# The outputs of 512-token tiles turned by VectorE and stored in pieces, gated by ScalarE when they come back

## The chip, the cores and the metric

The kernel runs on one core of a Trainium2 chip. The metric is the time of one launch on the device, in microseconds (us). Engines are named as in the profile: PE is TensorE's matmul, PEld its weight load, DVE VectorE, ACT ScalarE, POOL GpSimd and SP SyncE; a q behind a name (SPq) is that engine's own queue of instructions.

## The reference

A causal convolution along the sequence, done by Fourier transforms, and then a mixture of experts that takes one expert for each token:

```
x: 8 x 5696 x 128, h: 5696 x 128            # 45568 tokens in all
y = irfft(rfft(x, 2S) * rfft(h, 2S))[:, :S]  # per channel
logits = y @ w_gate + modality_bias[modality_id]
e_idx = argmax(logits); gate_w = softmax(logits)[e_idx]
for e in range(8):
    h = relu(y[e_idx == e] @ w1[e])          # 128 -> 1024
    out[e_idx == e] = gate_w * (h @ w2[e])   # 1024 -> 128
```

## The kernel before

The convolution is a chain of matmul stages (stage1, stage23, stage4). stage4 makes rows of y, works out expert and gate of each, and scatters every row with its gate and its token number to `rows` in HBM, sorted by expert. Tables (`table`) then cut these sorted rows into tiles: LEVELS comes out as 18, 18 and 45 tiles of 512 tokens (81 "big" tiles, three levels) and 23 slots for "small" tiles of 256 tokens, of which 20 always run and the last 3 only if they are needed.

`Moe.tiles` takes one tile after the other in steps: 8 steps for a big tile, 4 for a small one, each for 128 (big) or 256 (small) columns of the hidden layer. A step is `gemm1` (each product in three matmuls, high and low halves of the operands), ACT's relu into hh, DVE's rest into hl, and, two steps later (LAG = 2), `gemm2`, which sums into PSUM tile po. `prep` splits the next tile's input into mxh (ACT) and mxl (DVE). For a small tile PE first transposes the input into PSUM tile pxt; for nearly all big tiles DVE turns 32x32 blocks into mxt instead, and the load (four DMAs of 128-byte pieces) has put the blocks where they belong. `finish(t - 1)` runs at step 2 of tile t: PE transposes the output ot (copied from po by ACT) into pxt, DVE multiplies it by the gate into of. pxt is one buffer (the pool has bufs=1), for the transposes of `prep` and those of `finish`.

The first two levels run beside stage4 of the convolution, which still scatters rows on the same POOL queue, so their 36 tiles are not written out: `finish` stores them to `late` in HBM, and `bring` loads them back (tile ob) from tile 37 on. `scatter` sends 128 rows per DMA from POOL to the output, by token numbers in mmt or held; `evenly` spreads the scatters, one step at most one, each tied to the step's relu. Once the convolution has ended, `moe.alone` is set and the rest (from about tile 32 on) is recorded with PE in program order; SP is in program order all the while, and DVE, ACT and POOL go by the order that a scheduler chose.

SP issues weights (`load_weights`, three slots, only if the expert changes), inputs and stores in one queue. The input's gate and token numbers (mmt) have 5 buffers, and a buffer is free when the scatters that read their token numbers from it have landed.

Of the kernel before, what the change touches and what calls it, by code (L numbers as in the profile page):

```python
# [10 lines left out]
F32 = mybir.dt.float32  # L11
F32R = mybir.dt.float32r
BF16 = mybir.dt.bfloat16
# [46 lines left out]
LEVELS += ((NTOK - sum(LEVELS) * TS + E * (TSL - 1)) // TSL,)  # L60
NLAST = 3
NHELD = LEVELS[0] + LEVELS[1]
SMALL = LEVELS[3] - NLAST
EVEN = ((NHELD + LEVELS[2]) * NSUB + SMALL * TSL // 128) / (8 * (LEVELS[2] - 2) + 4 * (SMALL - 3))
JOBS = [(lv, j) for lv, n in enumerate(LEVELS) for j in range(n)]
OOB_ROW = 1 << 22
OOB_TOK = 1 << 20
# [24 lines left out]
def conv_moe(  # L92
# [234 lines left out]
    def stage4(g, sp, ps, psl, qa, qb, paced=False, late=None):  # L327
# [39 lines left out]
        for q0 in range(qa, qb, QB):  # L367
# [7 lines left out]
            for qi in range(QB):  # L375
                q = q0 + qi
                u = us.pop(q)
                load_u(q + 1)
                if not paced:
                    uh = sp.tile([128, 2, GC], F32R, name="uh")  # L380
                    ul = sp.tile([128, 2, GC], F32R, name="ul")
                    nc.scalar.copy(uh, u)
                    nc.vector.tensor_tensor(ul, u, uh.bitcast(F32), op=ALU.subtract)
                yield
                py = ps.tile([128, GC], F32, name="py")
                if paced:
# [12 lines left out]
                for b in range(GB):  # L399
                    nc.tensor.transpose(pt[:, b, :], ry[:, b, :], ident)  # L400
                if whole:
                    yt = sp.tile([128, GB, 128], F32, name="yt")
                    nc.scalar.copy(yt, pt)
                    yield
                    for b in range(GB):
                        t = qi * GB + b
                        nc.tensor.matmul(pl[:, t * E:(t + 1) * E], yt[:, b, :], wg, start=True, stop=True)  # L407
                else:
                    ys = [late.tile([128, GB, 128], BF16, name=f"ys{i}") for i in range(3)]
# [168 lines left out]
    class Moe:  # L578
        def __init__(self, wp, sp0, sp, pst, psh, pso):
            self.sp0, self.sp, self.pst, self.psh, self.pso = sp0, sp, pst, psh, pso  # L580
            self.slots = [wp[i].tile([128, 2, 2, FF], F32R, name=f"slot{i}") for i in range(NSLOT)]
            self.st, self.alone = {}, False
            self.outs = []
            self.tabs = {}
            self.held = wp[0].tile([128, NHELD, NSUB], I32, name="held")
            self.back, self.backs, self.credit = 0, [], 0.0

        def on_pe(self, t):
            return t < NPE or JOBS[t][0] == len(LEVELS) - 1
# [1 line left out]
        def load(self, t):  # L591
            lv, j = JOBS[t]
            tab, src = self.tabs[lv]
            ts = TSL if lv == len(LEVELS) - 1 else TS
            ns = ts // 128
            r0 = nc.sync.value_load(tab[0:1, j:j + 1], min_val=0, max_val=E * REGION)
            rt = self.sp0.tile([128, TS], F32, name="mrt", bufs=4)
            mt = self.sp0.tile([128, NSUB, 2], F32, name="mmt", bufs=5)
            if self.on_pe(t):
                nc.sync.dma_start(rt[:, :ts].rearrange("p (c d) -> p c d", d=D), src[bass.ds(r0, ts), :D].rearrange("(c p) d -> p c d", p=128))  # L600
            else:
                for j in range(0, D, BK):
                    nc.sync.dma_start(rt[j:j + BK, :ts].rearrange("p (n w) -> p n w", w=BK),
                                      src[bass.ds(r0, ts), j:j + BK].rearrange("(n p) w -> p n w", p=BK))
            nc.sync.dma_start(mt[:, :ns], src[bass.ds(r0, ts), D:].rearrange("(c p) w -> p c w", p=128))
            self.st[t] = {"rt": rt, "mt": mt, "ts": ts, "ns": ns}

        def load_weights(self, t):
# [6 lines left out]
        def prep(self, t):  # L615
            st = self.st[t]
            rt, ts, ns = st["rt"], st["ts"], st["ns"]
            xp, s = (self.sp, "") if t else (self.sp0, "0")
            if self.on_pe(t):
                px = self.pst.tile([128, NSUB, 128], F32, name="pxt")  # L620
                for c in range(ns):
                    nc.tensor.transpose(px[:, c, :], rt[:, c * D:(c + 1) * D], ident)
                pf = px.rearrange("p c t -> p (c t)")[:, :ts]
            else:
                pf = self.sp0.tile([128, TS], F32, name="mxt", bufs=1)[:, :ts]
                nc.vector.transpose(pf, rt[:, :ts])
            xh = xp.tile([128, TS], F32R, name="mxh" + s)
            xl = xp.tile([128, TS], F32R, name="mxl" + s)
            nc.scalar.copy(xh[:, :ts], pf)
            nc.vector.tensor_tensor(xl[:, :ts], pf, xh[:, :ts].bitcast(F32), op=ALU.subtract)  # L630
            st.update(xh=xh[:, :ts], xl=xl[:, :ts])

        def gemm1(self, t, f):
            w = self.slots[t % NSLOT]
# [16 lines left out]
        def gemm2(self, t, f):  # L651
# [13 lines left out]
                nc.tensor.matmul(po, w[:, 1, 1, fs], hh[:, cs], start=False, stop=False)  # L665
                nc.tensor.matmul(po, w[:, 1, 0, fs], hl[:, cs], start=False, stop=k == 7)  # L666
            if k == 7:
                ot = self.sp.tile([128, TS], F32, name="ot")
                nc.scalar.copy(ot[:, :ts], po)
                st["ot"] = ot  # L670

        def finish(self, t):
            st = self.st.pop(t)
            ns = st["ns"]
            pq = self.pst.tile([128, NSUB, 128], F32, name="pxt")
            for c in range(ns):
                nc.tensor.transpose(pq[:, c, :], st["ot"][:, c * 128:(c + 1) * 128], ident)  # L677
            of = self.sp.tile([128, NSUB, D], F32, name="of")
            rt = st["mt"]
            nc.vector.tensor_tensor(of[:, :ns], pq[:, :ns], rt[:, :ns, 0:1].to_broadcast([128, ns, D]), op=ALU.mult)  # L680
            ri = rt.bitcast(I32)
            if t < NHELD:
                nc.gpsimd.tensor_copy(self.held[:, t, :].unsqueeze(2), ri[:, :, 1:])
                nc.sync.dma_start(late_d[t], of.rearrange("p c d -> p (c d)"))
                return
            for c in range(ns):
                self.outs.append((t, c, ri[:, c, 1:2], of))

        def bring(self):
            if self.back < NHELD and len(self.backs) <= NSUB // 2:  # L690
                t = self.back
                self.back += 1
                of = self.sp.tile([128, NSUB, D], F32, name="ob")
                nc.sync.dma_start(of.rearrange("p c d -> p (c d)"), late_d[t])
                for c in range(NSUB):
                    self.backs.append((t, c, self.held[:, t, c:c + 1], of))

        def evenly(self, after):
            self.credit = min(self.credit + EVEN, 1.5)
# [24 lines left out]
        def tiles(self, first, total):  # L724
# [11 lines left out]
            for g in range(len(steps) + LAG):  # L736
# [5 lines left out]
                if t < total:  # L742
# [1 line left out]
                    dispatch(1, self.st[t]["act"])  # L744
                    self.evenly(self.st[t]["act"])
                    if t > NHELD:
                        self.bring()
                else:
                    self.scatter(1)
                if g >= LAG:  # L750
# [14 lines left out]
            while self.outs or self.backs or self.back < NHELD:  # L765
                self.scatter(len(self.outs))
                self.outs, self.backs = self.backs, []
                self.bring()
# [11 lines left out]
    with tc.tile_pool(name="p4l", bufs=1, space=PSUM) as ps4l:  # L780
# [19 lines left out]
        with tc.tile_pool(name="moe", bufs=2) as sp, tc.tile_pool(name="moew", bufs=1) as wp, \  # L800
# [120 lines left out]
```

## Time and profile before

| | us |
|---|---|
| median of 3 runs (2046.9 to 2052.02) | 2047.59 |
| the profiled execution's own time | 2045.59 |
| its span in the trace | 2043.8 |
| PE busy | 1962.4 (96%) |
| DVE busy | 1445.8 (71%) |
| ACT busy | 1133.6 (55%) |
| POOL busy | 1112.3 (54%) |

The tiles begin at about 808 us. The convolution ends at about 1350, big tiles at 1904, and the last matmul starts at 2031. Times in the trace count from the span's start. A matmul's duration covers its way through the array, and the next one starts before it ends; so what a matmul costs is read from one start to the next.

### The profile page before, as it was taken

How to read it: one execution, taken by the hardware profiler on the slowest of the kernel's cores; microseconds unless marked ns; L12 is line 12 of the kernel's file. 1: busy time of each engine (PE TensorE's matmuls, PEld its weight loads, DVE VectorE, ACT ScalarE, POOL GpSimd, SP SyncE). 2: the span in 40 equal slices, each digit the busy share in tenths (PEclk: the TensorE clock that was granted, in tenths of full speed). 3: DMA queues.
4: the chain of work that ended last, by engine and by line, in shares of the span. 5: the costliest groups of instructions: out<-in, count | busy, mean ns of one | idle time of the engine just before them, and what ended most of it. 6: DMA issues, size and time to landing. Idle time of an engine off the chain costs nothing. (4 is left out here: it accounts for less than half of the span.)

```text
span 2043.8 us, 32620 instructions
## 1 busy us (share of the span) xinstructions
PE 1962.4 (96%) x9114; PEld 1418.1 (69%) x9114; DVE 1445.8 (71%) x2478; ACT 1133.6 (55%) x2000; POOL 1112.3 (54%) x1085
## 2 busy tenths in 40 slices
PE   6889999999999899899999999999999999999996
PEld 5755555544544445778878778788888888888996
DVE  7759888886787897577676776866666666666553
ACT  5756777644444444566566666555555555555553
POOL 2117777673777685444444444633555555555554
PEclk8989999999999998999999999999999999999998
DMA  9998999979999997644456644354333343334443
GB/s 332 403 354 286 330 325 326 299 237 325 331 336 322 308 328 240 187 133 133 104 168 173 177 125 101 80 173 92 78 77 78 79 116 81 76 80 150 149 152 121
DMA packets 395832, 407.09 MB, mean 199 GB/s; under 512 B 242584, under 2 KB 277369, under 8 KB 393345
## 3 DMA queue, kind: packets, MB, share of 16 engines
q1 hardware_dynamic: 324496, 271.97, 44.7%
q10 hardware_dynamic: 47920, 85.94, 13.1%
q0 software_dynamic: 23232, 47.08, 6.7%
q8 instruction: 74, 1.21, 0.2%
q14 instruction: 110, 0.89, 0.1%
HBM read 396.70 MB, written 182.99 MB: 284 GB/s over the span
## 5 line engine op out<-in xcount | busy, mean ns | idle before, releaser
L320 POOL DMA_INDIRECT rows<-rt,idx x360 | 369.2, 1025 | 271.1 <-ACT hh L647 184.0
L648 DVE SCALAR_TENSOR_TENSOR hl<-ph,hh 128x512 fp32r<-128x512 f32 x496 | 338.0, 684 | 211.7 <-ACT hh L647 205.7
L647 ACT ACTIVATE hh<-ph 128x512 fp32r<-128x512 f32 x496 | 295.7, 598 | 278.3 <-PE ph L644 234.1
L290 POOL TENSOR_TENSOR t<-t,t 96x512 f32<-96x512 f32 x224 | 328.7, 1487 | 140.5 <-DVE t L283 119.9
L283 DVE TENSOR_TENSOR t<-px,hs 96x512 f32<-96x512 f32 x512 | 318.2, 676 | 68.3 <-PE px L280 29.5
L709 POOL DMA_INDIRECT out<-of,mmt x220 | 216.8, 985 | 216.4 <-ACT hh L647 186.7
L664 PE MATMUL po<-hh,slot 128*128 128x512 f32 (+1 forms) x808 | 304.3, 377 | 7.0 <-ACT hh L647 6.9
L666 PE MATMUL po<-hl,slot 128*128 128x512 f32 (+1 forms) x808 | 300.3, 372 | 0.3 <-DVE hl L648 0.3
L665 PE MATMUL po<-hh,slot 128*128 128x512 f32 (+1 forms) x808 | 299.5, 371 | 0.0
L280 PE MATMUL px<-z,m 96*96 96x512 f32 x512 | 256.1, 601 | 5.7 <-DMA z<-z 2.7
L648 DVE SCALAR_TENSOR_TENSOR hl<-py,hh 128x512 fp32r<-128x512 f32 x232 | 160.0, 690 | 105.2 <-ACT hh L647 105.0
L647 ACT ACTIVATE hh<-py 128x512 fp32r<-128x512 f32 x232 | 138.5, 597 | 164.2 <-PE py L644 152.1
L263 ACT COPY ut<-pu 90x512 f32<-90x512 f32 x256 | 147.9, 580 | 137.2 <-PE pu L258 69.1
L642 PE MATMUL ph<-mxh,slot 128*128 128x512 f32 (+1 forms) x536 | 210.7, 393 | 4.6 <-SPq L720 3.8
L258 PE MATMUL pu<-t,mi 96*96 96x512 f32 x384 | 199.0, 610 | 7.9 <-ACT ut L263 4.6
L644 PE MATMUL ph<-mxl,slot 128*128 128x512 f32 (+1 forms) x536 | 201.9, 377 | 0.0
L643 PE MATMUL ph<-mxh,slot 128*128 128x512 f32 (+1 forms) x536 | 201.9, 377 | 0.0
L709 POOL DMA_INDIRECT out<-ob,held x144 | 139.9, 971 | 109.6 <-ACT hh L647 90.6
L664 PEld LDWEIGHTS po<-hh,slot 128*128 128x128 f32 x808 | 152.8, 189 | 35.2 <-ACT hh L647 9.8
L666 PEld LDWEIGHTS po<-hl,slot 128*128 128x128 f32 x808 | 152.5, 189 | 28.3 <-DVE hl L648 0.9
L665 PEld LDWEIGHTS po<-hh,slot 128*128 128x128 f32 x808 | 152.8, 189 | 25.1
L280 PEld LDWEIGHTS px<-z,m 96*96 96x96 f32 x512 | 82.4, 165 | 119.8 <-issue 72.9
(173 smaller groups left out, 3464.0 us busy)
## 6 DMA issues: line engine op xcount, KB each, us to landing
slot<-w12s SPq DMA_DIRECT2D x101, 2048.0 KB
z<-z SPq DMA_DIRECT2D x128, 360.0 KB
z<-z SPq DMA_DIRECT2D x45, 640.0 KB
z<-z SPq DMA_DIRECT2D x45, 512.0 KB
mrt<-rows SPq DMA_DIRECT2D x312, 64.0 KB
w12s<-ws ACTq DMA_DIRECT2D x32, 512.0 KB
u<-ua ACTq DMA_DIRECT2D x63, 256.0 KB
u<-ub ACTq DMA_DIRECT2D x63, 256.0 KB
```

Of the source, the lines that this page charges most:

```text
L280: nc.tensor.matmul(px[:KP], mm, zbuf[k % NZ][:, i], start=True, stop=True)
L283: prods[0] = nc.vector.tensor_tensor(prod[i, j].rearrange("p (b d) -> p b d", d=D), px[:KP].rearrange("p (b d) -> p b d", d=D), hs[:, j, k ...
L290: add = eng.tensor_tensor(y[:, i], y[:, i], prod[1, 1 - i], op=ALU.add if i else ALU.subtract)
L320: d = nc.gpsimd.indirect_dma_start(views[count[0] % NVIEW], bass.IndirectOffsetOnAxis(ap=idx[:, t:t + 1], axis=0), rt[:, t, :], None, boun ...
L642: nc.tensor.matmul(po, w[:, 0, 0, fs], st["xh"], start=True, stop=False)
L643: nc.tensor.matmul(po, w[:, 0, 1, fs], st["xh"], start=False, stop=False)
L647: st["act"] = nc.scalar.activation(hh, ph, AF.Relu)
L648: nc.vector.scalar_tensor_tensor(hl, ph, 0.0, hh.bitcast(F32), op0=ALU.max, op1=ALU.subtract)
L664: nc.tensor.matmul(po, w[:, 1, 0, fs], hh[:, cs], start=k == 0, stop=False)
L665: nc.tensor.matmul(po, w[:, 1, 1, fs], hh[:, cs], start=False, stop=False)
L666: nc.tensor.matmul(po, w[:, 1, 0, fs], hl[:, cs], start=False, stop=k == 7)
L709: d = nc.gpsimd.indirect_dma_start(oviews[(t * NSUB + c) % NVIEW], bass.IndirectOffsetOnAxis(ap=ix, axis=0), of[:, c, :], None, bounds_che ...
```

## The change

The output of every big tile now goes through `late`, and PE transposes none of them. After the last `gemm2` of a big tile DVE turns po in 32x32 blocks into ot (one buffer), and `finish` stores ot with four DMAs, each of 32 partitions and 16 x 32 pieces of 128 bytes, so that `late` holds whole token rows. `bring` loads whole tiles back into the buffers that stage4 used for ys (four of them), and `gate` lets ACT multiply one block of 128 rows a step by its gate, in place, from 8 steps after the load was asked for. Gate and token numbers of big tiles stay in the tiles near and held; those of small tiles have 8 buffers. Small tiles are finished as before. When the tiles run alone, `prep` is cut into `turn`, `high` and `low`, recorded in three steps that follow each other, and DVE and ACT keep program order too.

```
+            near = wp[0].tile([128, NEAR, NSUB, 2], F32, name="near")
+            held = sp.tile([128, NBIG - NEAR, NSUB, 2], F32, name="held", bufs=1)
+            self.meta = [near[:, t] if t < NEAR else held[:, t - NEAR] for t in range(NBIG)]
...
-            mt = self.sp0.tile([128, NSUB, 2], F32, name="mmt", bufs=5)
+            mt = self.meta[t] if t < NBIG else self.sp0.tile([128, TSL // 128, 2], F32, name="mmt", bufs=8)
...
             if k == 7:
-                ot = self.sp.tile([128, TS], F32, name="ot")
-                nc.scalar.copy(ot[:, :ts], po)
-                st["ot"] = ot
+                ot = st["ot"] = self.sp.tile([128, TS], F32, name="ot", bufs=1)[:, :ts]
+                if t < NBIG:
+                    nc.vector.transpose(ot, po)
+                else:
+                    nc.scalar.copy(ot, po)
 
         def finish(self, t):
             st = self.st.pop(t)
             ns = st["ns"]
+            if t < NBIG:
+                for j in range(0, D, BK):
+                    nc.sync.dma_start(late_d[t].rearrange("(n p) d -> p n d", p=BK)[:, :, j:j + BK],
+                                      st["ot"][j:j + BK].rearrange("p (n w) -> p n w", w=BK))
+                return
             pq = self.pst.tile([128, NSUB, 128], F32, name="pxt")
...
+        def bring(self, t):
+            if self.back < min(NBIG, t - 1) and len(self.ripe) + len(self.backs) < (NOB - 1) * NSUB:
+                yb = self.sp.tile([128, 3, GB, 128], BF16, name="ys", bufs=NOB)
+                ob = yb.rearrange("p i b t -> p (i b t)").bitcast(F32)[:, :TS].rearrange("p (c d) -> p c d", d=D)
+                nc.sync.dma_start(ob.rearrange("p c d -> p (c d)"), late_d[self.back].rearrange("(p c) d -> p (c d)", c=NSUB))
+                self.ripe += [[AGE, self.back, c, ob] for c in range(NSUB)]
                 self.back += 1
...
+        def gate(self, after=None):
+            for it in self.ripe:
+                it[0] -= 1
+            while self.ripe and (after is None or self.ripe[0][0] < 0):
+                _, t, c, ob = self.ripe.pop(0)
+                mt = self.meta[t]
+                m = nc.scalar.activation(ob[:, c], ob[:, c], AF.Copy, scale=mt[:, c, 0:1])
+                self.backs.append((t, c, mt.bitcast(I32)[:, c, 1:2], ob))
+                if after is not None:
+                    tc.add_manual_dep(m.ins, after.ins.name, PACED, reason="order")
+                    break
...
                 if t + 1 < total:
-                    if f == (4 if n == 8 else 0):
-                        self.prep(t + 1)
+                    parts = (self.turn, self.high, self.low)
+                    if not self.alone:
+                        if f == (4 if n == 8 else 0):
+                            self.prep(t + 1)
+                    elif f - (3 if n == 8 else 0) in range(3):
+                        parts[f - (3 if n == 8 else 0)](t + 1)
...
-            with tc.manual_schedule(engines={mybir.EngineType.PE}):
+            with tc.manual_schedule(engines={mybir.EngineType.PE, mybir.EngineType.Activation, mybir.EngineType.DVE}):
                 run_all((tiles, 1))
```

How it stands on three engines (rows of before carry its line numbers, rows of the changed kernel its own). First PE at step 2 of a big tile that runs alone, from `gemm1` (into ph) over `gemm2` (into po) to the next step's `gemm1` (into py). Before:

```order
L642 MATMUL ph_22789<-mxh_22681,slot2_7161 128x512
L643 MATMUL ph_22789<-mxh_22681,slot2_7161 128x512
L644 MATMUL ph_22789<-mxl_22682,slot2_7161 128x512
L664 MATMUL po_22800<-hh_22728,slot2_7161 128x512
L665 MATMUL po_22800<-hh_22728,slot2_7161 128x512
L666 MATMUL po_22800<-hl_22729,slot2_7161 128x512
L677 MATMUL pxt_22804<-ident_67,ot_22752 128x128 x4
L642 MATMUL py_22811<-mxh_22681,slot2_7161 128x512
```

The same place in the changed kernel:

```order
L660 MATMUL ph_22364<-mxh_22251,slot0_7159 128x512
L661 MATMUL ph_22364<-mxh_22251,slot0_7159 128x512
L662 MATMUL ph_22364<-mxl_22252,slot0_7159 128x512
L682 MATMUL po_22378<-hh_22303,slot0_7159 128x512
L683 MATMUL po_22378<-hh_22303,slot0_7159 128x512
L684 MATMUL po_22378<-hl_22304,slot0_7159 128x512
L660 MATMUL py_22386<-mxh_22251,slot0_7159 128x512
```

The four transposes of the tile before are gone, and nothing stands in their place.

Next DVE over one small tile. hl are the steps' rests, mxl the low half of the next tile's input (read from pxt, where PE's `turn` of step 0 put it), of the gated output of the tile before (read from pxt, too). Before, from one mxl to the next:

```order
L630 TENSOR_TENSOR mxl_25009<-pxt_25005,mxh_25008 128x256
L648 SCALAR_TENSOR_TENSOR hl_25020<-py_25012,hh_25019 128x512
L648 SCALAR_TENSOR_TENSOR hl_25076<-ph_25068,hh_25075 128x512
L680 TENSOR_TENSOR of_25092<-pxt_25089,mmt_24562 128x256
L648 SCALAR_TENSOR_TENSOR hl_25102<-py_25094,hh_25101 128x512
L648 SCALAR_TENSOR_TENSOR hl_25122<-ph_25114,hh_25121 128x512
L630 TENSOR_TENSOR mxl_25135<-pxt_25131,mxh_25134 128x256
```

And in the changed kernel, from the hl of step 3 to the hl of step 3 of the next tile:

```order
L666 SCALAR_TENSOR_TENSOR hl_23783<-py_23775,hh_23782 128x512
L666 SCALAR_TENSOR_TENSOR hl_23803<-ph_23795,hh_23802 128x512
L666 SCALAR_TENSOR_TENSOR hl_23823<-py_23815,hh_23822 128x512
L666 SCALAR_TENSOR_TENSOR hl_23881<-ph_23873,hh_23880 128x512
L644 TENSOR_TENSOR mxl_23871<-pxt_23812,mxh_23870 128x256
L705 TENSOR_TENSOR of_23899<-pxt_23896,mmt_23353 128x256
L666 SCALAR_TENSOR_TENSOR hl_23909<-py_23901,hh_23908 128x512
```

mxl stood behind the hl of step 0 and now stands behind the hl of step 2, directly ahead of of; PE's transposes for of stand at the end of step 2 in both kernels, and write the pxt that mxl reads.

Last POOL at its end, ahead of the branch to the three slots that may not be needed (of are blocks of small tiles, ob and ys those of big ones). Before:

```order
L709 DMA out<-of_25672,mmt_25189 45568x128
L709 DMA out<-ob_25403,held_7162 45568x128 x2
L709 DMA out<-of_25760,mmt_25316 45568x128 x2
L709 DMA out<-of_25802,mmt_25442 45568x128 x2
L719 TENSOR_LOAD tab3_15729
```

And in the changed kernel:

```order
L741 DMA out<-of_25716,mmt_25266 45568x128 x2
L741 DMA out<-ys_25103,held_7163 45568x128
L741 DMA out<-ys_24722,held_7163 45568x128 x2
L741 DMA out<-of_25758,mmt_25391 45568x128 x2
L741 DMA out<-ys_25103,held_7163 45568x128 x2
L751 TENSOR_LOAD tab3_15492
```

Two blocks of a big tile now stand behind the last small tile's two.

## Rows read from the trace of the kernel before

**Rows 1.** The page's first part: busy time, share of the span and instructions.

```profile
PE 1962.4 (96%) x9114; PEld 1418.1 (69%) x9114; DVE 1445.8 (71%) x2478; ACT 1133.6 (55%) x2000; POOL 1112.3 (54%) x1085
```

**Rows 2.** Busy time by stretch, then PE's granted clock, DMA share, GB/s.

```profile
830.00:1350.00 520.00, 518.11 (x2833) 417.56 (x2833) 374.22 (x804) 322.73 (x581) 260.51 (x304) 1.00 0.51 138
1350.00:1904.00 554.00, 553.68 (x2525) 454.54 (x2524) 348.03 (x530) 284.78 (x484) 290.08 (x297) 1.00 0.39 95
1904.00:2014.00 110.00, 109.46 (x925) 109.26 (x924) 62.90 (x107) 55.21 (x106) 56.53 (x59) 1.00 0.50 161
```

**Rows 3.** Timeline of PE in a big tile: start, duration, what.

```profile
1501.66 0.39 PE L666 MATMUL po<-hl,slot 128*128 128x512 f32 x1
1501.89 0.60 PE L677 MATMUL pxt<-ident,ot 128*128 128x128 f32 x4
1502.24 0.48 PE L642 MATMUL py<-mxh,slot 128*128 128x512 f32 x1
1502.56 0.39 PE L643 MATMUL py<-mxh,slot 128*128 128x512 f32 x1
```

**Rows 4.** The chain that ended last: start, us, what; 43 tiles' transposes, first, last.

```profile
1410.19 0.44 PE pxt L677 x4
...
1891.88 0.44 PE pxt L677 x4
```

**Rows 5.** Timeline of all engines in a small tile.

```profile
1988.75 0.42 DVE L630 TENSOR_TENSOR mxl<-pxt,mxh 128x256 fp32r<-128x256 f32 x1
...
1990.17 0.28 PE L644 MATMUL ph<-mxl,slot 128*128 128x256 f32 x1
...
1990.49 0.60 ACT L647 ACTIVATE hh<-ph 128x512 fp32r<-128x512 f32 x1 [0.35 <-PE ph L644]
...
1991.02 0.38 PE L677 MATMUL pxt<-ident,ot 128*128 128x128 f32 x2
...
1991.13 0.69 DVE L648 SCALAR_TENSOR_TENSOR hl<-ph,hh 128x512 fp32r<-128x512 f32 x1 [0.75 <-ACT hh L647]
```

**Rows 6.** Timeline of PE around its two gaps among the small tiles.

```profile
1985.56 0.28 PE L666 MATMUL po<-hl,slot 128*128 128x256 f32 x1
1986.38 0.39 PE L642 MATMUL ph<-mxh,slot 128*128 128x256 f32 x1 [0.54 <-DMA slot<-w12s]
1986.61 0.28 PE L643 MATMUL ph<-mxh,slot 128*128 128x256 f32 x1
...
2017.16 0.28 PE L666 MATMUL po<-hl,slot 128*128 128x256 f32 x1
2021.27 0.58 PE L642 MATMUL ph<-mxh,slot 128*128 128x256 f32 x1 [3.82 <-SPq L720]
...
2024.63 0.31 PE L642 MATMUL py<-mxh,slot 128*128 128x256 f32 x1
```

**Rows 7.** Timeline of SP's queue: one input of a big tile; the last weights.

```profile
1501.57 1.93 SPq L603 DMA_DIRECT2D mrt<-rows  x4
...
2010.22 0.38 SPq L605 DMA_DIRECT2D mmt<-rows  x1
2012.50 0.35 SPq L613 DMA_DIRECT2D slot<-w12s  x1
```

**Rows 8.** SP's waits, 1904 to 2034 us: us in total, times, longest.

```profile
SPq L605 <- DMA out<-of,mmt: 27.3, 12, 6.4
```

**Rows 9.** Groups by shape, 1060 to 2044 us: count, busy us, mean ns, idle before.

```profile
L626 DVE STREAM_TRANSPOSE mxt<-mrt 128x512 f32<-128x512 f32 x64 | 44.9, 702 | 2.2 <-DMA mrt<-rows 2.1
L451 ACT ACTIVATE ex<-lg 128x96 f32<-128x96 f32 x10 | 2.9, 295 | 1.0 <-DVE lg L436 0.9
```

**Rows 10.** Timeline of POOL at its end.

```profile
2032.05 0.97 POOL L709 DMA_INDIRECT out<-of,mmt  x1 [0.72 <-DVE of L680]
2033.33 0.97 POOL L709 DMA_INDIRECT out<-of,mmt  x1 [0.30 <-issue]
```

**Rows 11.** DMA queues, 1400 to 1900 us: packets, MB, share of 16 engines.

```profile
q1 hardware_dynamic: 114454, 25.46, 27.0%
```

More of the change, by code (lines that the diff above doesn't have):

```diff
@@ L62 @@
 NHELD = LEVELS[0] + LEVELS[1]
+NBIG = NHELD + LEVELS[2]
+NEAR = 4
+AGE = 7
+NOB = 4
 SMALL = LEVELS[3] - NLAST
-EVEN = ((NHELD + LEVELS[2]) * NSUB + SMALL * TSL // 128) / (8 * (LEVELS[2] - 2) + 4 * (SMALL - 3))
+EVEN = (NBIG * NSUB + SMALL * TSL // 128) / (8 * (LEVELS[2] - 2) + 4 * (SMALL - 3))
 JOBS = [(lv, j) for lv, n in enumerate(LEVELS) for j in range(n)]
@@ L408, in stage4 @@
                 else:
-                    ys = [late.tile([128, GB, 128], BF16, name=f"ys{i}") for i in range(3)]
+                    yb = late.tile([128, 3, GB, 128], BF16, name="ys", bufs=NOB)
+                    ys = [yb[:, i] for i in range(3)]
                     yr = sp.tile([128, GB, 128], F32, name="yt")
@@ L584, in __init__ @@
             self.tabs = {}
-            self.held = wp[0].tile([128, NHELD, NSUB], I32, name="held")
-            self.back, self.backs, self.credit = 0, [], 0.0
+            near = wp[0].tile([128, NEAR, NSUB, 2], F32, name="near")
+            held = sp.tile([128, NBIG - NEAR, NSUB, 2], F32, name="held", bufs=1)
+            self.meta = [near[:, t] if t < NEAR else held[:, t - NEAR] for t in range(NBIG)]
+            self.back, self.ripe, self.backs, self.credit = 0, [], [], 0.0
         def on_pe(self, t):
@@ L622, in prep, with high, low @@
                     nc.tensor.transpose(px[:, c, :], rt[:, c * D:(c + 1) * D], ident)
-                pf = px.rearrange("p c t -> p (c t)")[:, :ts]
+                st["pf"] = px.rearrange("p c t -> p (c t)")[:, :ts]
             else:
-                pf = self.sp0.tile([128, TS], F32, name="mxt", bufs=1)[:, :ts]
+                pf = st["pf"] = self.sp0.tile([128, TS], F32, name="mxt", bufs=1)[:, :ts]
                 nc.vector.transpose(pf, rt[:, :ts])
[L627 to L631, printed above, removed]
+        def high(self, t):
+            st = self.st[t]
+            xp, s = (self.sp, "") if t else (self.sp0, "0")
+            st["xh"] = xp.tile([128, TS], F32R, name="mxh" + s)[:, :st["ts"]]
+            st["xl"] = xp.tile([128, TS], F32R, name="mxl" + s)[:, :st["ts"]]
+            nc.scalar.copy(st["xh"], st["pf"])
+        def low(self, t):
+            st = self.st[t]
+            nc.vector.tensor_tensor(st["xl"], st["pf"], st["xh"].bitcast(F32), op=ALU.subtract)
+        def prep(self, t):
+            self.turn(t)
+            self.high(t)
+            self.low(t)
         def gemm1(self, t, f):
@@ L677, in finish @@
                 nc.tensor.transpose(pq[:, c, :], st["ot"][:, c * 128:(c + 1) * 128], ident)
-            of = self.sp.tile([128, NSUB, D], F32, name="of")
+            of = self.sp.tile([128, TSL // 128, D], F32, name="of")
             rt = st["mt"]
-            nc.vector.tensor_tensor(of[:, :ns], pq[:, :ns], rt[:, :ns, 0:1].to_broadcast([128, ns, D]), op=ALU.mult)
+            nc.vector.tensor_tensor(of, pq[:, :ns], rt[:, :ns, 0:1].to_broadcast([128, ns, D]), op=ALU.mult)
             ri = rt.bitcast(I32)
[L682 to L685, printed above, removed]
@@ L686, in finish @@
             for c in range(ns):
                 self.outs.append((t, c, ri[:, c, 1:2], of))
-        def bring(self):
-            if self.back < NHELD and len(self.backs) <= NSUB // 2:
-                t = self.back
-                self.back += 1
[L693 to L696, printed above, removed]
+        def bring(self, t):
[4 more added lines that the diff above has]
+                self.ripe += [[AGE, self.back, c, ob] for c in range(NSUB)]
+                self.back += 1
@@ L746, in tiles @@
                     if t > NHELD:
-                        self.bring()
+                        self.gate(self.st[t]["act"])
+                        self.bring(t)
                 else:
@@ L764, in tiles @@
                 self.finish(total - 1)
-            while self.outs or self.backs or self.back < NHELD:
+            while self.outs or self.backs or self.ripe or self.back < NBIG:
                 self.scatter(len(self.outs))
+                self.gate()
                 self.outs, self.backs = self.backs, []
-                self.bring()
+                self.bring(total)
     fx = ExitStack()
@@ L914 @@
     args.append(scratch("w12s", (E, 128, 2, 2, FF)))
-    args.append(scratch("late", (NHELD, 128, TS)))
+    args.append(scratch("late", (NBIG, TS, D)))
     args.append(nc.dram_tensor("out", (NTOK, D), F32, kind="ExternalOutput").ap())
```

6 lines of the change are left out of this document (3 added, 3 removed).

## The prediction

> **What bounds the kernel now.** I read the page's busy times first: PE is busy for 96% of the span, no other engine for more than 71% [rows 1]. As a busy PE need not be a PE at its peak, the table by stretch comes next: beside the convolution, in the big tiles that run alone and in the small tiles PE has at most 0.4% idle, at a granted clock of 1.00, the 2.4 GHz level [rows 2]. So from 830 us to 2014 us the end is set by the list of PE's instructions, and the reader is to see that an instruction taken off that list is worth its full pitch until something new makes PE wait. The pitch is in the timeline: in a big tile L677's four transposes start 0.23 us after the matmul ahead of them, and the second matmul behind them starts 0.67 us after they do, where 0.23 is usual; so the four cost 0.44 us [rows 3]. The chain of waits gives the same 0.44 to each, and a period of (1891.88 - 1410.19) / 42 = 11.47 us a tile [rows 4]; the other 48 matmuls at 0.23 make 11.04.
>
> **What goes.** 81 big tiles lose these transposes: 81 x 0.44 = 35.6 us (28 if only the distance to the next matmul's start, 0.35, is saved; 38 at 0.47).
>
> **What the big tiles get in exchange.** DVE turns po instead of multiplying: the block transpose of an input of the same size takes 0.70 us [rows 9]; the place of the multiplication is free for it. ACT gets one gating of 128x128 a step and loses the copy of ot. Such a gating isn't in the trace; 128x96 takes 0.295 us [rows 9], so I take 0.3, with 0 and the 0.60 of a 128x512 relu [rows 5] as its ends. A step lasts 11.47 / 8 = 1.43 us and holds one relu, 0.60 + 0.30 of ACT's time, and even 1.20 fits. In program order each DVE step carries hl (0.69) and at most one more instruction of 0.70, 1.39 in a step of 1.43 (1.38 without the transposes); a surplus of 0.01 passes on to the next step, which carries hl alone, and hl is wanted two steps later; that hides it. SP issues four more DMAs a tile, 1.93 us by the four of an input [rows 7], and one to two loads; it has about 3 us of work in 11.47. The pieces of a store are as small as those of an input. Queue q1's packets took 27.0% of 16 engines over 500 us, 114454 of them: 0.27 x 500 x 16 / 114454 = 18.9 ns each [rows 11]. A store of 2048 pieces then takes 2048 x 18.9 ns / 16 = 2.4 us of the 16 DMA engines (nothing to 4.8 us if a written piece costs twice). The mean DMA share of 0.39 is 4.5 us a tile [rows 2]; with 2.4 and about 1 us more of loads it is 7.9 of 11, so the stores stay hidden. What is left are three or four weight loads between the big tiles, behind which a load of ys can be late and hold ACT at its gate, and the start of the stage alone: 0 to 6 us, I take 1.
>
> **What the small tiles get.** Here the order matters more than the work. pxt is one buffer. Before, DVE read its share of it at 1988.75 to 1989.17, and PE wrote the finished tile's transposes into it at 1991.02, straight behind its matmuls [rows 5]. In the changed order mxl stands behind step 2's hl, and PE's transposes, at the end of the same step, must wait for mxl. The same rows give the times: that step's last `gemm1` matmul starts at 1990.17, hh follows at 1990.49, hl at 1991.13 and takes 0.69, then mxl 0.42: 1992.24, against 1991.02. PE waits 1.2 us in each tile where `low` of the next and `finish` of a small one meet, tiles 82 to 99: 18 x 1.2 = **21.6 us** lost (20 if DVE overlaps the two, 29 if ACT's gate, ot and mxh delay hh by 0.4; nothing if I misread the order). Behind PE's transposes stand all later matmuls, so nothing covers it; ACT and DVE then wait for those.
>
> **What SP gives back.** PE has two gaps among the small tiles, both at weights. Matmuls follow each other at 0.12; from 1985.56 to 1986.38 there are 0.7 us too many, from 2017.16 to 2021.27 there are 4.0 [rows 6]. The weights of the second were issued at 2012.50, 2.3 us behind an mmt load [rows 7] which waits for scatters; such waits cost SP 27.3 us in 12 times, up to 6.4 [rows 8]. With 8 buffers for small tiles alone they go, and the longer tiles give the weights two times 1.2 us more. From 2021.27 to 2024.63 PE starts 15 matmuls, 0.22 each where 0.12 is usual: the level of 1.2 GHz, 3.36 - 15 x 0.12 = 1.6 us. Together 0.7 + 4.0 + 1.6 = 6.3 us returned (bounds 0 and 6.3).
>
> **The tail.** In the new POOL order two blocks stand behind the last small tile's. POOL's last scatters start 1.28 apart [rows 10]: 2.6 us. Up to eight blocks of big tiles have no step to pace them, so the bounds are 0 and 10.
>
> **The sum.** 2045.6 (the profiled execution's own time) - 35.6 + 1 + 21.6 - 6.3 + 2.6 = 2028.9. The median of the runs shown is 2.0 above that execution, so **2031 us**; its own range is 2020 to 2041. That is 0.8% less, half of what the removed transposes alone would bring. 0.3% of 2047.59 is 6.1 us, about what a measurement of this kernel can tell from no change.
>
> **Rivals.**
>
> *No wait at pxt.* If mxl is done in time after all, the 21.6 stays: 2045.6 - 35.6 + 1 - 5 + 2.6 + 2.0 = **2011**. For it: DVE is busy for only 62.9 of 110 us there [rows 2], and mxh is ready a step earlier. Against it: program order leaves DVE no choice, and hl cannot start ahead of hh. Chance 0.22.
>
> *The pieces are too slow* (slower than before). ot has one buffer, and DVE may not write it until the store has read it, 11 us later. SP issues the store behind the input's DMAs, some 6 us after the tile's last matmul, which leaves about 5 us for 2.4. Up to twice the price per piece, 4.8, nothing happens; at 8 us DVE would come 3 us late in 49 tiles alone, less 1.5 of slack: 2031 + 73 = **2104**. A gain of 16.8 is used up when each of the 49 loses 0.34 us, at a store of about 7 us. For it: no row has a written piece of 128 bytes. Against it: read pieces and the rest of q1 average 18.9 ns [rows 11]. Chance 0.08. The Trainium skill speaks against this step of the change: DMA: Bandwidth & Descriptors, Specifications, puts the least transfer for line rate at 512 bytes and says that below this the DMA does a read-modify-write. By that rule a written piece would cost more than a read one; at twice, an estimate from that page's words, the store takes 4.8 us and the sum stays as it is, and no run here shows the price.
>
> *The clock falls among the small tiles.* A small tile is 4 steps of 12 matmuls at 0.12, 5.8 us, and two pairs of transposes, some 6.1; a wait of 1.2 us per tile takes PE to 84% busy. After the 4 us gap the clock was halved and 1.6 us were lost; after the 0.7 us gap the matmul behind the next started 0.23 later and the pace was 0.12 again [rows 6]. If each of the 18 waits cost half clock as the long gap did: 2031 + 18 x 1.6 = **2060**; 0.9 us per wait takes the gain away. Chance 0.10.
>
> *Late loads.* If the back-loads come late often and ACT's gate holds hh, or the stores disturb the stage beside the convolution (DMA share 0.51 [rows 2]), 5 to 20 us are lost: about **2043**. Chance 0.08.
>
> **How the numbers follow.** The forecast has 0.52; the four rivals have 0.22, 0.08, 0.10 and 0.08. The range from 2007 to 2044 takes in the first rival, the forecast and about half of the late loads, 0.78, and leaves the two costly ones out. Faster by over 0.3% (below 2041.4): 0.51 of the forecast, 0.22 of the first rival, 0.03 of the late loads and 0.02 of the clock, where it costs little: 0.78. Slower (above 2053.7): 0.05 of the pieces, 0.05 of the clock and 0.01 of the loads: 0.11. The same takes the rest, 0.11.
>
> **What would show it.** Period of the big tiles alone 11.0 us and no L702 transposes in them; in the small tiles L702 idle 1.2 us, released by DVE's mxl (L644), 18 times, and a period of about 7.3 us, not 6.1; no gap at weights near the end; two scatters of ys after the last of. A gate L724 of about 0.3 us. The prediction is wrong if L702 does not wait, if DVE's turn of po (L688) waits for DMAs of late, if the relu waits for a gate held by a load, or if the granted clock among the small tiles is below 1.00.

## The result, and the profile after

The changed kernel takes 2062.01 us (median of 5 runs) where the kernel before takes 2047.59: a ratio of 1.0063, 95% interval 1.0045 to 1.0081. It is slower, by 14 us, where 17 less were forecast. The profiled execution took 2062.42 us, 16.8 more than the one before.

The page's first part, to be held against [rows 1]:

```profile
PE 1937.7 (94%) x8790; PEld 1388.4 (67%) x8790; DVE 1448.0 (70%) x2478; ACT 1213.0 (59%) x2243; POOL 1108.3 (54%) x1049
```

PE has 324 matmuls less and 24.7 us less to do, yet the span is longer: PE waits now. Where, the table by stretch tells (columns as in [rows 2]; the last stretch is longer than before, up to the last small tiles):

```profile
830.00:1350.00 520.00, 513.79 (x2724) 410.70 (x2724) 375.75 (x811) 313.00 (x559) 260.95 (x272) 0.99 0.58 140
1350.00:1904.00 554.00, 537.68 (x2373) 440.58 (x2372) 355.75 (x536) 372.80 (x737) 285.34 (x292) 0.99 0.64 140
1904.00:2031.00 127.00, 107.79 (x874) 104.81 (x873) 59.40 (x101) 60.34 (x128) 55.90 (x58) 0.99 0.43 136
```

PE idles 16.3 us in the middle stretch, where it had 0.3, and 19.2 us in the last. There the kernel before has 4.8, most of it the gap of 3.82 at 2021 [rows 6]:

```profile
1904.00:2031.00 127.00, 122.17 (x1015) 121.56 (x1014) 68.40 (x116) 60.22 (x115) 65.21 (x68) 0.99 0.48 158
```

The two stretches have different shapes. In the middle one it is three waits and a quiet rest. PE's timeline, at the first two of them and then at the third, among the first small tiles:

```profile
1362.13 0.39 PE L683 MATMUL po<-hh,slot 128*128 128x512 f32 x1
1368.52 0.79 PE L684 MATMUL po<-hl,slot 128*128 128x512 f32 x1 [6.00 <-DVE hl L666]
1369.11 0.63 PE L660 MATMUL py<-mxh,slot 128*128 128x512 f32 x1
...
1658.46 0.50 PE L684 MATMUL po<-hl,slot 128*128 128x512 f32 x1 [1.90 <-DVE hl L666]
...
1901.56 0.66 PE L702 MATMUL pxt<-ident,ot 128*128 128x128 f32 x2 [7.25 <-DVE mxl L644]
```

The releasers named, hl and mxl, are only the last link. One step further back, the timelines of DVE and of ACT show who really waited:

```profile
1358.62 0.69 DVE L666 SCALAR_TENSOR_TENSOR hl<-py,hh 128x512 fp32r<-128x512 f32 x1 [0.70 <-ACT hh L665]
1367.17 0.72 DVE L688 STREAM_TRANSPOSE ot<-po 128x512 f32<-128x512 f32 x1 [7.86 <-DMA late<-ot]
1367.81 0.65 DVE L666 SCALAR_TENSOR_TENSOR hl<-ph,hh 128x512 fp32r<-128x512 f32 x1
...
1899.21 0.37 ACT L690 COPY ot<-po 128x256 f32<-128x256 f32 x1 [5.96 <-DMA late<-ot]
```

DVE's turn of po stands at the head of DVE's order until the store of the tile before has read ot, and hl stands behind it. At 1899 it is ACT's copy of the first small tile that wants the same buffer; ACT's next hh stands behind that copy, DVE's hl needs that hh, and mxl stands behind hl. Asked who waited for ot, the trace has these two rows for the stores, in us and times:

```profile
  DVE ot L688: 17.8, 6
  ACT ot L690: 6.0, 1
```

SP's queue shows why that store is late. Its work before the first of the waits:

```profile
1345.07 2.16 SPq L697 DMA_DIRECT2D late<-ot  x4
1349.29 8.23 SPq L867 DMA_DIRECT2D rows<-padt  x8
1359.36 0.11 SPq L621 DMA_DIRECT2D slot<-w12s  x1
1360.47 1.97 SPq L610 DMA_DIRECT2D mrt<-rows  x4
1362.63 0.59 SPq L613 DMA_DIRECT2D held<-rows  x1
1363.27 2.23 SPq L697 DMA_DIRECT2D late<-ot  x4
```

The store of 1363.27 should have gone out near 1356, 11 us after the one of 1345.07; the eight pad rows (8.2 us of SP's time, issued once when the convolution ends) and one tile's weights and rows stand ahead of it. Before the second wait it is other work:

```profile
1643.85 0.34 SPq L621 DMA_DIRECT2D slot<-w12s  x1
1644.98 2.81 SPq L610 DMA_DIRECT2D mrt<-rows  x4
1647.99 4.51 SPq L613 DMA_DIRECT2D held<-rows  x1
1652.60 2.22 SPq L697 DMA_DIRECT2D late<-ot  x4
```

Here the expert changes, and 2 MB of weights go out (0.34 us; where the expert stays, as at 1359.36, L621 takes 0.11). Behind them the issue of 4 KB into held keeps SP for 4.51 us, where it took 0.59 at 1362.63. From 1340 us on only four of these issues last over 1 us, and each stands behind weights. Before the third wait it is other work again:

```profile
1887.13 0.37 SPq L621 DMA_DIRECT2D slot<-w12s  x1
1888.63 0.40 SPq L607 DMA_DIRECT2D mrt<-rows  x1
1889.24 0.58 SPq L613 DMA_DIRECT2D mmt<-rows  x1
1894.28 0.34 SPq L714 DMA_DIRECT2D ys<-late  x1
1894.72 2.09 SPq L697 DMA_DIRECT2D late<-ot  x4
```

From 1889.82 to 1894.28 SP issues nothing: the back-load L714 waits for a ys buffer that POOL's scatters still read, and the store stands behind it. In the list of SP's waits from 1350 to 1904 us this is the first row (us in total, times, longest):

```profile
SPq L714 <- DMA out<-ys,held: 85.7, 45, 4.3
```

Between these waits the big tiles run as forecast, with no transposes in them: from tile 36 to tile 59 their starts gain 10.3 us on those of before, 0.45 a tile. The small tiles, against [rows 5]:

```profile
1984.52 0.60 ACT L665 ACTIVATE hh<-ph 128x512 fp32r<-128x512 f32 x1
...
1984.91 0.28 PE L684 MATMUL po<-hl,slot 128*128 128x256 f32 x1
...
1985.15 0.69 DVE L666 SCALAR_TENSOR_TENSOR hl<-ph,hh 128x512 fp32r<-128x512 f32 x1 [0.73 <-ACT hh L665]
...
1985.76 0.41 DVE L644 TENSOR_TENSOR mxl<-pxt,mxh 128x256 fp32r<-128x256 f32 x1
...
1986.32 0.41 PE L702 MATMUL pxt<-ident,ot 128*128 128x128 f32 x2 [1.13 <-DVE mxl L644]
```

The wait at pxt is there, released by mxl behind hl, as the order said: 17 waits of 1.12 to 1.17 us, 19.3 in all, and an eighteenth hidden in the wait of 7.25. A small tile takes 7.46 us from start to start, 6.16 before. No gap at weights is left ([rows 6] had 4.7 us), and SP's wait for scatters at the small tiles' mmt loads ([rows 8]) is gone. POOL's end, against [rows 10]:

```profile
2045.07 0.98 POOL L741 DMA_INDIRECT out<-of,mmt  x1 [0.30 <-issue]
2046.35 0.98 POOL L741 DMA_INDIRECT out<-of,mmt  x1 [0.30 <-issue]
2048.86 0.97 POOL L741 DMA_INDIRECT out<-ys,held  x1 [1.53 <-DMA out<-of,mmt]
2050.14 0.98 POOL L741 DMA_INDIRECT out<-ys,held  x1 [0.30 <-issue]
```

Two ys scatters stand behind the last of, but they come late: POOL had been working back to back at 1.28 us since 2025.7. From PE's last matmul to the end of the span it is 19.4 us, 12.5 before.

### The profile page after: what moved, and what is told of

The parts are those of the page before. It is cut to its first block, busy times and chain, and to the rows that moved or that the text cites. A ratio compares the mean times of both kernels' runs of the same rounds, so it can differ in the third digit from the quotient of the medians.

```text
span 2060.6 us, 32585 instructions
## 1 busy us (share of the span) xinstructions
PE 1937.7 (94%) x8790; PEld 1388.4 (67%) x8790; DVE 1448.0 (70%) x2478; ACT 1213.0 (59%) x2243; POOL 1108.3 (54%) x1049
## 3 DMA queue, kind: packets, MB, share of 16 engines
q8 instruction: 72, 1.18, 0.2%
## 5 line engine op out<-in xcount | busy, mean ns | idle before, releaser
L324 POOL DMA_INDIRECT rows<-rt,idx x360 | 375.2, 1042 | 301.7 <-ACT hh L665 222.6
L741 POOL DMA_INDIRECT out<-ys,held x308 | 301.0, 977 | 223.9 <-ACT hh L665 199.2
L724 ACT ACTIVATE ys<-ys,held 128x128 f32<-128x128 f32 x308 | 124.0, 403 | 10.1
```

Source lines behind the costliest of these rows:

```text
L324: d = nc.gpsimd.indirect_dma_start(views[count[0] % NVIEW], bass.IndirectOffsetOnAxis(ap=idx[:, t:t + 1], axis=0), rt[:, t, :], None, boun ...
L741: d = nc.gpsimd.indirect_dma_start(oviews[(t * NSUB + c) % NVIEW], bass.IndirectOffsetOnAxis(ap=ix, axis=0), of[:, c, :], None, bounds_che ...
```

## The experiments

The runs were made on three chips, each with the kernel before beside them. It took 2048.22 us on the chip of e5 to e8 and 2047.75 on that of e9 to e12. On the chip of e1 to e4 it took 2072.89 us (11 runs), and all four of these lay at 2089 and more, whatever their edit; so three edits were run again. Where e9 to e12 are held against e5 or e8, it is by the ratio to the kernel before.

**Two buffers for ot (e1, e6).** The edit takes the fourth buffer of mrt for the room:

```
-            rt = self.sp0.tile([128, TS], F32, name="mrt", bufs=4)
+            rt = self.sp0.tile([128, TS], F32, name="mrt", bufs=3)
-                ot = st["ot"] = self.sp.tile([128, TS], F32, name="ot", bufs=1)[:, :ts]
+                ot = st["ot"] = self.sp.tile([128, TS], F32, name="ot", bufs=2)[:, :ts]
```

> After the change, with two buffers for the turned outputs ot in place of one (and three for the raw rows mrt in place of four, to make room; the fourth was never waited for). Theory (one ot buffer, its store late behind other work of SP's queue): the three places where ot waited for its store lose their waits: 7.2 us on PE near 1368, 1.9 near 1658, about 9 around 1901, so about 2044 us, 18 less than the changed kernel's 2062; tile starts 36 to 59 move by -7, 61 to 77 by -9, the small tiles by -18. The small tiles' waits of 1.1 us on mxl stay. Rival (the pieces cost through the load on the DMA engines, which slows whatever is in flight): nothing of it is recovered, 2058 to 2064.

Measured: 2092.56 us, a ratio of 1.011 (1.0088 to 1.0133), on the chip of 2072.89. The waits for ot were gone there, but ACT paused in a way that no run on the other chips had. Its timeline, with PE's output complete at 1462.3:

```profile
1461.55 0.40 ACT L724 ACTIVATE ys<-ys,held 128x128 f32<-128x128 f32 x1
1464.45 0.60 ACT L665 ACTIVATE hh<-ph 128x512 fp32r<-128x512 f32 x1 [2.49 <-PE py L662]
```

From 1395 to 1900 us 49 relus came more than 2 us after the one before, mostly 10 to 14 of ACT's instructions after the last such stop; in the changed kernel's own profile there are three, at waits that the trace names. So the time of this run says nothing on the theory.

**The exchange of the small tiles in one step (e2).**

```
-                    if not self.alone:
+                    if not self.alone or n == 4:
                         if f == (4 if n == 8 else 0):
                             self.prep(t + 1)
```

> After the change, with the small tiles' exchange (turn, high, low) issued in one step, as it was before the change, and not in three. Theory (the 17 waits of 1.12 to 1.17 us at the transposes of the outputs are for mxl, which DVE's program order puts behind hl): they go, 17 x 1.14 = 19 us, so about 2043 us, and the period of a small tile is about 6.2 us again. Rival (POOL's scatters, 1.28 us each and about 3.5 a tile, are the bound behind them): PE's gain comes back at the end as a longer tail of scatters; 10 us or more of the 19 are lost there, 2053 to 2062. The big tiles stay as they were, with the three long waits.

Measured: 2091.58 us, 1.0096 (1.0067 to 1.0126), same chip, same stops of ACT. No L702 waits for mxl any more; the size of the effect is read from e7.

**Whole rows in the store (e3, e9).** The kernel leaves out putting each value in its place in late.

```
-                for j in range(0, D, BK):
-                    nc.sync.dma_start(late_d[t].rearrange("(n p) d -> p n d", p=BK)[:, :, j:j + BK],
-                                      st["ot"][j:j + BK].rearrange("p (n w) -> p n w", w=BK))
+                nc.sync.dma_start(late_d[t].rearrange("(p c) d -> p (c d)", c=NSUB), st["ot"])
```

> After the change, with a big tile's output stored by one transfer of 128 rows of 2 KB in place of four with 2048 pieces of 128 bytes (so each value lies in another place of late, and the rows of the output are permuted). ot keeps its one buffer and the store its place in SP's queue. Theory (place in the queue and the single buffer): the store ends 1 to 1.5 us earlier, and of the three waits that together cost 18 us some 3 to 5 go: 2056 to 2059. Rival (the pieces themselves: the longer transfers and the load on the DMA engines): the waits go, and the mixed stage gets back some 6 us: 2035 to 2045.

Measured on the same chip: 2089.65 us, 1.0094 (1.006 to 1.0128); not to be read.

**The store ahead of the loads (e4, e10).** The four lines that issue weights and rows move behind `finish`, to the step `f == LAG`:

```
-                if f == (LAG - 1 if t else 5):
-                    if t + 2 < total:
-                        self.load_weights(t + 2)
...
                 if f == LAG and first <= t - 1:
                     self.finish(t - 1)
+                if f == (LAG if t else 5):
+                    if t + 2 < total:
+                        self.load_weights(t + 2)
...
```

> After the change, with SP's order turned in a step of each tile: first the store of the last tile's output, then the weights two tiles ahead and the rows three tiles ahead, one step (1.4 us) later than now. One ot buffer, pieces as they are. Theory (the store is late because weights and rows, 4 to 9 us of SP's time, stand before it): the waits near 1658 and 1901 go (1.9 and about 9 us), the one near 1368 keeps the pad rows ahead of it and falls from 7 us to about 3: 2046 to 2050 us. Rival (the rows and weights come one step later and are missed): new waits at mrt or the weights, no less than 2062.

Measured on the same chip: 2110.58 us, 1.0202 (1.0173 to 1.0231); not to be read either.

**The changed kernel again (e5),** unaltered, on another chip:

> The changed kernel itself, unaltered, as the measure for the others of this call. In the four runs before, ACT stood for about 2.3 us after every 11 or 12 of its instructions from the stage of big tiles on, with the output of PE ready (for example 1461.95 to 1464.45 in the run with two ot), and the kernel before took 2073 there and not 2048. Theory (it belongs to the chip and the run, not to the edits): where the kernel before takes about 2048, this one takes 2062 and ACT does not stand; where it takes about 2073, this one takes 2090 or more and ACT stands in the same way. Rival (the edits themselves make ACT stand): this one is 2062 or so whatever the kernel before takes.

Measured: 2059.90 us, 1.0063 (1.005 to 1.0077), beside 2048.22. ACT does not pause, and the waits are those of the first profile (6.00, 1.61 and 7.18 us, then 17 of 1.12 to 1.17). That the pauses belong to that chip, or to its state at the time, is supported by e1 and e6, one kernel with and without them; what makes ACT pause was not found, and the kernel before was not profiled there.

> The kernel of the first run again (two buffers for ot, three for mrt), beside the unaltered changed kernel. Theory (one ot buffer, stores late behind other work of SP): 18 us less than the unaltered changed kernel, the waits of 7.2, 1.9 and about 9 us gone. Rival (load on the DMA engines): the same as the unaltered one within 3 us.

Measured: 2036.03 us, 0.9947 (0.9929 to 0.9965): 23.9 us less than e5. The theory holds; that 6 us more came than it said is in good part chance. The first tile of the profiled executions starts at 809.44 us in e5 and at 805.86 in e6, where this edit has no part (e7, the same program up to the small tiles, starts at 811.44). From there to the end of the span e6 is 18.3 us shorter, the 18 of the theory. The three waits alone sum to less than that; the time at half clock behind the long ones went with them, and the tile with the 6.00 us wait is 8.2 us shorter. The list of who waited for ot has no L688 or L690 left. In the table by stretch the 2.3 us that PE idles in 546 are two waits of small tiles (1.17 and 1.12) at the row's end, so the big ones have none; the small ones keep theirs, now 18 of 1.12 to 1.18:

```profile
1340.00:1886.00 546.00, 543.71 (x2437) 447.56 (x2436) 362.41 (x544) 378.35 (x748) 287.92 (x295) 1.00 0.65 144
1886.00:2005.00 119.00, 100.78 (x831) 98.00 (x830) 56.06 (x96) 56.57 (x119) 54.30 (x56) 1.00 0.44 142
```

The DMA engines are as loaded as before this edit (0.65), so their load was not the cause.

**Both edits (e7).**

> Two buffers for ot and the small tiles' exchange in one step, together. Theory (the two losses add up): 18 + 19 = 37 us less than the unaltered changed kernel, 22 less than the kernel before (2025 where it takes 2048). Rival (POOL's scatters bound the small tiles, so that their gain comes back in the tail): 20 to 27 us less than the unaltered changed kernel.

Measured: 2018.95 us, 0.9855 (0.9839 to 0.9872): 40.9 us less than e5, 17.1 less than e6. They add up. (Counted from the first tile, the profiled execution is 21.5 us shorter than that of e6 and 39.8 shorter than that of e5.) The waits at pxt are gone; one small gap at weights is back (1.77 us at 1960). What did not shrink is the tail: 19.1 us from PE's last matmul to the end of the span.

**A faster drain (e8).** With e7's edits, and

```
-EVEN = (NBIG * NSUB + SMALL * TSL // 128) / (8 * (LEVELS[2] - 2) + 4 * (SMALL - 3))
+EVEN = (NBIG * NSUB + SMALL * TSL // 128) / (8 * (LEVELS[2] - 2) + 4 * (SMALL - 3)) * 1.05
```

> As the run before this in the list, with EVEN times 1.05, so that the scatters of the big tiles are through five small tiles before the end and only the last outputs follow PE's last matmul (8 fewer at the end). Theory (POOL's backlog of 1.28 us a scatter makes the tail 19.8 us and not 13): 5 to 8 us less than without it. Rival (the tail is the fixed latency of the last scatters, and POOL has no slack in the stage of big tiles for more of them): no change, or up to 4 us more.

Measured: 2010.57 us, 0.982 (0.9803 to 0.9837), 8.4 less than e7. POOL is through with the big tiles in time, and its end is the last outputs alone:

```profile
1992.12 0.98 POOL L741 DMA_INDIRECT out<-of,mmt  x1 [2.94 <-DVE of L705]
1993.40 0.98 POOL L741 DMA_INDIRECT out<-of,mmt  x1 [0.30 <-issue]
1995.61 0.98 POOL L741 DMA_INDIRECT out<-of,mmt  x1 [1.23 <-DVE of L705]
1996.89 0.98 POOL L741 DMA_INDIRECT out<-of,mmt  x1 [0.30 <-issue]
```

Before the first of these POOL waits for DVE: there is no queue left. The tail is 12.5 us, 6.6 less. In the table by stretch PE is the bound again, idle for 0 in 537 and 1.1 in 113:

```profile
1340.00:1877.00 537.00, 537.00 (x2374) 440.71 (x2373) 358.28 (x537) 378.79 (x751) 300.33 (x308) 1.00 0.66 147
1877.00:1990.00 113.00, 111.94 (x946) 111.54 (x945) 63.52 (x108) 61.77 (x123) 53.78 (x56) 1.00 0.49 158
```

**Pieces or place in the queue (e9, e10).**

> The changed kernel with a big tile's output stored by one transfer of 128 rows of 2 KB (each value lies in another place of late, the rows of the output are permuted), again, on a chip where ACT does not stand: counted from the unaltered changed kernel (1.0063 of the kernel before). One ot buffer, the same place in SP's queue. Theory (the store is late because of what stands before it on SP): the store is 1 to 1.5 us shorter, and of the 24 us that a second buffer gave at most 8 come: a ratio of 1.002 to 1.005. Rival (the pieces are what costs): all 24 come, a ratio of 0.995 or lower.

Measured: 2058.60 us, 1.0057 (1.0039 to 1.0075), against 1.0063: no difference that can be told. The waits are 5.40 us at 1361 and 6.91 at 1892, where e5 has 6.00 and 7.18; only the middle one (1.61) went. So the pieces were not what cost; the theory holds. By the medians the gain is smaller even than the 3 to 8 us it granted; from the first tile on the profiled execution is 3.9 us shorter than that of e5.

> The changed kernel with SP's order turned within a tile (store of the last output, then weights and rows, one step later than now), again, counted from 1.0063. Theory (the place in SP's queue): the waits near 1658 and 1898 go, the one near 1365 keeps the pad rows ahead of it: 12 to 20 us less, a ratio of 0.997 to 1.001. Rival (rows and weights a step later are missed): new waits at mrt or the weights of the small tiles, a ratio of 1.006 or more.

Measured: 2055.70 us, 1.0043 (1.0026 to 1.006), 4 us less where 12 to 20 were expected. PE's three rows:

```profile
1364.08 0.50 PE L684 MATMUL po<-hl,slot 128*128 128x512 f32 x1 [3.34 <-DVE hl L666]
...
1889.92 0.41 PE L702 MATMUL pxt<-ident,ot 128*128 128x128 f32 x2 [2.35 <-DVE mxl L644]
...
1896.01 0.55 PE L660 MATMUL ph<-mxh,slot 128*128 128x256 f32 x1 [3.95 <-DMA slot<-w12s]
```

The first wait behaves as the theory said (the pad rows stay ahead), the one near 1655 is gone, and the one at the first small tile falls from 7.18 to 2.35, since a back-load that waits still stands ahead of that store. Right behind it comes a new wait of 3.95 us for weights that were issued a step later. Both sides were half right: the place in the queue makes the store late, and with one queue an earlier store is a later load.

**Order on the engines, and pieces without the wait (e11, e12),** both against e8. In e11 the last `manual_schedule` names PE alone:

```
-            with tc.manual_schedule(engines={mybir.EngineType.PE, mybir.EngineType.Activation, mybir.EngineType.DVE}):
+            with tc.manual_schedule(engines={mybir.EngineType.PE}):
```

> The best version (two ot, exchange of small tiles in one step, EVEN times 1.05; 0.982 of the kernel before) with only PE in program order at the end, ACT and DVE placed by the scheduler as before the change. Theory (program order as such is neither gain nor loss, once the small tiles' exchange is in one step): within 4 us of the best version. Rival 1 (program order is what keeps hh and hl on time beside the gates): 5 to 30 us more, with waits of PE on hh or hl. Rival 2 (program order still holds something up): 4 us or more less.

Measured: 2011.84 us, 0.9829 (0.9808 to 0.9851), against 0.982: the same. Program order on ACT and DVE shows neither gain nor loss, once the small tiles' exchange is in one step.

> The best version (0.982 of the kernel before) with whole rows of 2 KB in place of the pieces in the store (values at other places of late, rows of the output permuted). Theory (with two buffers the store has a tile's period, and nothing waits for its pieces): within 3 us of the best version. Rival (the 1856 more packets a tile of q1 slow other transfers that are waited for, or the mixed stage): 4 us or more less.

Measured: 2011.16 us, 0.9815 (0.9796 to 0.9835): the same. The two traces also give the price of a written piece, since only the store differs. Queue q1 from 1400 to 1850 us, in e8 and then in e12 (packets, MB, share of 16 engines):

```profile
q1 hardware_dynamic: 203504, 44.64, 53.1%
```

```profile
q1 hardware_dynamic: 122560, 44.36, 43.4%
```

The difference is 0.097 x 450 x 16 = 698 us of engine time for the 41 x 128 = 5248 rows of 2 KB that 16 pieces each replace: 133 ns a row. By this difference a piece costs 133 / 16 = 8.3 ns and a sixteenth of what a whole row costs. The traces also hold each DMA packet with its size. Those of 128 bytes on q1 in the same 450 us take 13.7 ns in the mean in e8, where half of them are written pieces, and 14.0 ns in e12, where all are read. So a written piece costs no more than a read one.

## Why the prediction was wrong

**The step that failed** is "so the stores stay hidden", in the big tiles' exchange. The sum had 1 us (0 to 6) for it; a second buffer gave back 23.9 (e6 against e5), 18.3 of it from the first tile on. The reasoning compared two averages, 2.4 us of transfer and 5 us left, and the average was right: with one ot buffer most stores are in time. It missed that SP is one queue in order, and that what stands ahead of a store is not the same in every tile. The eight pad rows come once, weights of 2 MB come ahead of some stores, and a back-load that finds no free ys buffer holds SP for up to 4.3 us; the order of all three was in the program to be read. Where they fall, DVE or ACT waits up to 7.9 us for ot, hl or mxl stands behind it and PE stops. One of the prediction's own signs of being wrong, L688 waiting for DMAs of late, is what came. The rival of the slow pieces named the very mechanism (one buffer, DVE late) but with the wrong cause, the price of a piece; e9 and e12 show that this price does not decide, and the waits of e10 (3.34, none and 2.35 us for 6.00, 1.61 and 7.18) that the place in the queue does. The rule that spoke against the change there (the Trainium skill, DMA: Bandwidth & Descriptors, Specifications: below 512 bytes the DMA does a read-modify-write) did not show as a higher price here: 13.7 ns where half of the pieces are written, 14.0 where none is. Both lie below the 18.9 of [rows 11], which is a mean over packets of all sizes.

**The transposes' price.** 0.44 us a tile was right in the stage alone (0.45). Beside the convolution the gain was 8.2 us by tile 33 where 33 x 0.44 = 14.5 was due; e5 and e6, which start that stage 2.8 and 6.3 us earlier, gain 8.5 and 7.9 in it. So some 6 us are lost there in every version, without the waits for ot. The pieces are little of it: with whole rows (e9, e12) the gain is 9.5 and 9.1. PE's busy time fell from 518.11 to 513.79 of 520 us there. Some of the loss is PE waiting for ACT in stage4: from 830 to 1345 us these waits come to 4.1 us in e5 (2.6 at L404, 1.5 at L411) and to 1.4 in the kernel before (L400). What holds ACT up there, and where the rest goes, was not tried out.

**The wait at pxt** was right in kind, place, releaser and size: 17 waits of 1.14 for 18 of 1.2 (e6 has all 18), 19.3 us for 21.6. A tile loses 1.3 us by it, a little more than the wait. Undoing it gave 17.1 (e7 against e6), and 21.3 in the profiled executions from the first small tile to PE's last matmul.

**What SP gives back** was right: no gap at weights, no halved clock at the end.

**The tail** was undersized: 2.6 was forecast, 19.4 - 12.5 = 6.9 more came than before. The two scatters behind the last of were foreseen, the queue ahead of them was not, since POOL was taken to keep pace. EVEN is such that it does not quite: e8 gives 8.4 us back with 5% more, 6.6 of it in the tail.

**The clock** did not fall for waits of 1.14 us: 1.00 among the small tiles of e6, with PE busy for 100.78 of 119 us. It did fall in the waits of 6 and 7.25 us: behind them the granted clock is 0.50, the 1.2 GHz level, from 1368.5 to 1371 and from 1901.6 to 1907. Behind the 1.90 us wait it is 1.00.

**Two smaller readings.** The gate (L724) takes 0.40 us, not 0.3, and PE's idle time in the small tiles before is 0.5% (0.54 of 110 us in [rows 2]), not at most 0.4%. Nothing hangs on either.

The miss of 33.5 us (16.8 measured, -16.7 forecast), stage by stage in the two profiled executions: 6.3 beside the convolution, 19.2 from there to PE's last matmul and 4.3 in the tail. The 19.2 are the stores, since e6 needs 20.4 less in that stretch. Another 3.6 lie in the start of the tiles, which came that much later in this execution and between 2.7 earlier and 2.8 later in those of e5 to e8; that part is chance.

The gain was there all the same: with a second buffer, the exchange in one step and the faster drain the same change is 1.8% faster than the kernel before (2010.57 against 2048.22).

## What to carry to other kernels

Before a buffer is left single because its mean slack is enough, list what the store's queue issues ahead of it in every tile, the rare things and the waits of its own above all: three tiles out of fifty are enough to stop the engine that is the bound. When a load and a store share a queue, moving one forward moves the other back; a second buffer does not. When work is taken off the bound engine, look at the next queue in line (here POOL's scatters, at 1.28 us each) and pace it so that it is empty at the end.

## What was not expected of the hardware

On one chip ACT paused every 10 to 14 instructions, mostly for 1 to 3 us: in e1 49 relus from 1395 to 1900 us came more than 2 us after the one before, and the kernel before took 2072.89 us there and not 2048. The profiles from the other chips show nothing of the kind. An unaltered control on the same chip keeps this from being read as the edit: the second buffer, which gained 0.5% on the kernel before in e6, seemed to lose 1.1% there.

The issue of a small DMA can hold SP for long: behind 2 MB of weights the 4 KB into held took 1.9 to 5.5 us to issue, 0.57 in the median of this stage.

Whole rows of 2 KB instead of 128-byte pieces lowered the share of the DMA engines from 53.1% to 43.4% and the time by nothing.
